# Pair 1 of a gated layer with seven down products, a normalisation moved to ScalarE, and four pages for stores

## The chip, the cores and the metric

The kernel runs on one core of one Trainium2 chip. The metric is the device time of one execution, in microseconds (us). Before the change the median of three runs is 809.46 us (809.42 to 809.92).

## The reference, cut to what matters

```
x  = A_x                                    # 2048 x 512
xn = (x - mean(x)) / sqrt(var(x) + 1e-5)    # along the 512
a, b = xn @ Wd_re.T, xn @ Wd_im.T           # 512 x 512
s  = Ws_re @ a - Ws_im @ b                  # 2048 x 2048
h  = sigmoid(xn @ w_gate) * (xn @ w_up)     # 512 x 1792, twice
g  = silu(h @ w_down)                       # 1792 x 512
out = x + s * g
```

All is fp32. The kernel is given x also turned (`x_t`), and writes its output turned.

## The kernel before, in words

Each fp32 operand is split into a high part (a copy to fp32r on ScalarE, line 71) and a low part (a subtraction on VectorE, line 72), and each product is three matmuls (`mm3`, lines 75 to 77). Most matrix products are done as 2 x 2 blocks with seven block products in place of eight, from sums and differences of blocks that VectorE makes (line 123, `combine`).

The 1792 columns of the gated layer are seven groups of 256, called pairs; the 2048 rows are two halves h of 1024. A *block* (h, g) is one pair for one half. `BLOCKS` (line 28) gives their order: `start` does (0, 0), and (0, 1) (0, 2) (0, 3) (0, 4) (1, 4) ... follow. A block (`block`, line 443) is seven *units*, one for each of the products 1, 5, 2, 6, 7, 4, 3 that make gate and up together; a unit is 12 matmuls of 512 columns, into PSUM banks ga, gb, gc (gate) and ua, ub, uc (up). Chain a is used by products 1, 6, 7, 4; between them ScalarE copies banks away: `snap` (line 454) after product 6, which is position 3 of the block, and after product 7, position 4. `gate` (line 469) is the sigmoid, `times` (line 472) its product with up, `plus` (line 464) adds bank c.

The product with `w_down` (the *down* of a block) runs during the next block, item by item, at the end of units, into the two banks pd. There are two ways. `Plain` (line 313) has 4 items at positions 1, 3, 4, 6, each 2 outputs x 2 halves x 3 matmuls. `Seven` (line 387) has 7 items, one at each unit, each 2 outputs x 3 matmuls; it needs more operands: four sums of gated blocks, seven splits of them, and `Down` (line 359): four differences of quarters of the weights and two splits of 1024. `late` makes `Down.spread` (line 382) come four units later. In the kernel before, the first half uses `Plain` for pairs 1 and 2 and `Seven` from pair 3 on (`SEVEN_FROM`, line 30); the second half uses `Seven` throughout. The down of a block is stored at once: `gather` (line 297) copies the two banks with ScalarE (line 301) into a page, and GpSimd's queue stores the page to the DRAM tile `g_part`, adding if something is there (line 303).

The first half of x is normalised in `start`. For the second half (tiles 8 to 15 of 128 rows, i >= KH), `norm_a` (line 156) makes the statistics on VectorE (lines 160, 161) and mean and scale on GpSimd (lines 165 to 167) into the tile `moments`; `norm_b` (line 170) normalises the tile on VectorE (line 172); `store_xn` (line 196) stores it to `xn_part` from GpSimd's queue. The same rows are needed turned: `turned_half` (line 174) stores the moments to DRAM (`m_part`, line 182), loads them spread over all partitions, loads the turned x, and applies subtraction and product on VectorE (line 187) in four steps for each of two blocks of 512 columns. `x_sum` (line 236) makes the sums of these for the second half.

What sets the order: the whole program is written in the order of the units, and each engine and queue runs its own instructions in that order. In the loop at line 1013, unit n first runs what `sooner(n, ..)` holds, then starts the loads that units up to n + 5 need (SP's queue), makes the split operands that units up to n + 2 need, issues its matmuls, and then runs what `after(n, ..)` holds. Here unit 0 is the first of block (0, 1); block (0, 2) is units 7 to 13, (0, 3) units 14 to 20, and `turned_at` (line 989) is unit 28. The places of the second half's work are numbers in lines 991 to 1005.

All working tiles in SBUF come from one pool of 54 *pages* of 4 KB a partition (line 43): loads, splits, sums, and what is stored. A page that is given again is waited for by its first writer until the last reader, a store among them, is through.

After the gated layer come the two DFTs (`seq_units`, `hidden_units`). `silu_ahead` (line 718) makes silu of `g_part` in two pages, and `snap` in `after_product` (line 797) copies banks of the sequence DFT.

Of the kernel before, what the change touches and what calls it, by code (L numbers as in the profile page):

```python
# [9 lines left out]
F32 = mybir.dt.float32  # L10
F32R = mybir.dt.float32r
AF = mybir.ActivationFunctionType
ALU = mybir.AluOpType
# [9 lines left out]
NT = S // 512  # L23
SB = 512
EPS = 1e-5
PAGES = 54
SCRATCH = 4096
BLOCKS = ((0, 1), (0, 2), (0, 3), (0, 4), (1, 4), (1, 5), (0, 5), (0, 6), (1, 6), (1, 0), (1, 1), (1, 2), (1, 3))
FIRST_TURNED = 1, 4
SEVEN_FROM = 3  # L30
SHARED = 4, 5, 6
SPLIT_AHEAD = 2
LOAD_AHEAD = 5

# [2 lines left out]
def fnet_glu_kernel(ctx: ExitStack, tc: tile.TileContext, x, x_t, c_re, c_im, w_h, w_gu, w_down, out):  # L37
# [3 lines left out]
    const = ctx.enter_context(tc.tile_pool(name="const", bufs=1))  # L41
    stat = ctx.enter_context(tc.tile_pool(name="stat", bufs=4))
    pages = ctx.enter_context(tc.tile_pool(name="pages", bufs=PAGES))
    dram = ctx.enter_context(tc.tile_pool(name="dram", bufs=1, space=bass.MemoryType.DRAM))
    banks = ctx.enter_context(tc.tile_pool(name="banks", bufs=1, space=PSUM))

    def page(shape, dtype=F32R):
        return pages.tile([P, *shape], dtype, name="page")

    def bank(tag):  # L50
        return banks.tile([P, 512], F32, name=tag, bufs=2 if tag == "pd" else 1)
# [6 lines left out]
    nc.gpsimd.memset(mhalf, -0.5)  # L58
    warm = const.tile([P, 1], F32, name="warm")
    nc.scalar.activation(warm, mhalf, AF.Sigmoid)  # L60
    moments = const.tile([P, 2, KH], F32, name="moments")
    m_part = dram.tile([2, 2, SB], F32, name="m_part")
    xn_part = dram.tile([2, 2, 2, P, 4, D // 2], F32, name="xn_part")
    g_part = [dram.tile([P, 2, SB], F32, name=f"g_part{i}") for i in range(2 * NT)]
# [91 lines left out]
    def norm_a(i):  # L156
        st = stat.tile([P, 6], F32, name="st")
        mv = stat.tile([P, 2], F32, name="mv")
        rs = stat.tile([P, 2], F32, name="rs")
        nc.vector.bn_stats(st, xs[i])  # L160
        nc.vector.bn_aggr(mv, st)
        mean, scale = mv[:, 0:1], rs[:, 1:2]
        if i >= KH:
            mean, scale = (moments[:, m, i - KH : i - KH + 1] for m in range(2))
            nc.gpsimd.tensor_scalar(mean, mv[:, 0:1], 0.0, None, op0=ALU.add)
        nc.gpsimd.tensor_scalar(rs[:, 0:1], mv[:, 1:2], EPS, None, op0=ALU.add)
        nc.gpsimd.tensor_tensor(scale, rs[:, 0:1], mhalf, op=ALU.pow)
        st_of[i] = mean, scale

    def norm_b(i):  # L170
        mean, scale = st_of.pop(i)
# [124 lines left out]

    def gather(i, outs, sign=1):

        pg = page([2, SB], F32)
        for o, po in enumerate(outs):  # L300
            nc.scalar.activation(pg[:, o, :], po, AF.Copy, scale=float(sign))  # L301
        if i in begun:
            nc.gpsimd.dma_start(g_part[i], pg, accum_op=ADD)  # L303
        else:
            begun.add(i)
            nc.gpsimd.dma_start(g_part[i], pg)
# [410 lines left out]

    def silu_ahead(n, i):
        g = Load(g_part[i], [2, SB])
        t = Value([g], lambda: page([2, SB], F32))  # L720

        def give():
            nc.gpsimd.dma_start(gs_part[i], combine(t.get(), t.get(), g.load(), ALU.mult))

        sooner(n, g.load)
        after(n + 2, lambda: nc.scalar.activation(t.get(), g.load(), AF.Sigmoid))
        after(n + 3, give)

    def seq_units(job, c_sums):
# [8 lines left out]
        for tc_ in range(NT):  # L738
# [29 lines left out]
            def after_product(k, n=n, tc_=tc_, ps=ps, s=s, made=made, first=first, tags=tags):  # L768
                def put(blk):
                    half, j = blk // 2 ^ 1, blk % 2  # L770
                    to = f_part[tc_ // 2, half]
                    if tc_ % 2 == 0 or j:
                        nc.gpsimd.dma_start(to[SLOT["ab"[j] if tc_ % 2 == 0 else 3]], made[blk])
                    if tc_ % 2 == 0 or j == 0:
                        return
                    a1, b1 = made[blk - 1], made[blk]
                    t2 = []

                    def total(k):
                        a0, b0 = (first[half, j].load() for j in range(2))  # L780
                        if k == 6:
                            t2.append(page([2, SB], F32))
                        v = {
                            5: lambda: combine(a0, a0, a1, ADD),
                            7: lambda: combine(a1, a1, b1, ADD),
                            6: lambda: combine(t2[0], a0, b1, ADD),
                            4: lambda: combine(b0, t2[0], b0, ADD),
                        }[k]()
                        nc.gpsimd.dma_start(to[SLOT[k]], v)

                    at = n + 25 if half == 0 else n + 28 + (9 if tc_ < NT - 1 else 4)
                    for j in range(2):
                        sooner(at - 4 + j, first[half, j].load)
                    for i, k in enumerate((5, 7, 6, 4)):
                        after(at + i, lambda k=k: total(k))

                def snap(name, ch):
                    s[name] = page([2, SB], F32)
                    for d in range(2):
                        nc.scalar.activation(s[name][:, d, :], ps[ch, d], AF.Copy)  # L800
                    return s[name]

                def join(blk, name, ch, op, swap=False):
                    made[blk] = v = s[name]
                    for d in range(2):
                        x, y = v[:, d, :], ps[ch, d]
                        nc.vector.tensor_tensor(v[:, d, :], *((y, x) if swap else (x, y)), op=op)
                    put(blk)

                if k == 1:  # L810
                    for d in range(2):
                        ps["b", d] = bank("gu"[d] + tags["b"])
                        nc.scalar.activation(ps["b", d], ps["a", d], AF.Copy)
                elif k == 5:
                    snap("u5", "c")
                elif k == 6:
                    snap("u2", "a")
                elif k == 3:
                    join(2, "u2", "c", SUB)
                elif k == 7:  # L820
                    join(3, "u5", "a", SUB, swap=True)
                elif k == 2:
                    made[0] = snap("u1", "b")
                    put(0)
                else:
                    made[1] = snap("u4", "a")
                    put(1)
# [151 lines left out]
    with tc.manual_schedule():  # L979
# [4 lines left out]
        for h, g in BLOCKS:  # L984
# [2 lines left out]
                w, wd, last = w_operands(g), Down(g), g  # L987
            if (h, g) == FIRST_TURNED:
                turned_at = len(units)
            job = block(h, w, made, job, Seven(h, wd, made) if h or g >= SEVEN_FROM else Plain(h, g), g in SHARED)  # L990
        for i in range(0, KH, 2):
            a, b = ((2, 9), (4, 10), (7, 12), (8, 14))[i // 2]
            if i >= 4:
                sooner(a - 4, lambda i=i: fetch(KH + i))
            for j in (i, i + 1):
                after(a, lambda j=j: norm_a(KH + j))
                after(b, lambda j=j: norm_b(KH + j))
                after(b + 1, lambda j=j: store_xn(KH + j))
        n = turned_at
        turned_half(4, 0, (n - 18, n - 17, n - 14, n - 4))  # L1000
        turned_half(8, 1, (n - 13, n - 12, n - 10, n - 3))
        for i, k in {-7: 1, -2: 2, 0: 3, 2: 4}.items():
            after(n + i, lambda k=k: x_sum(1, k))
        for i, k in {-8: 1, -5: 5, -2: 2, 0: 6, 1: 7, 3: 4}.items():
            sooner(n + i, xop[1, k].get)
# [72 lines left out]
```

## Time and profile before

| | |
|---|---|
| median of three runs | 809.46 us (809.42 to 809.92) |
| profiled execution: its own time | 809.49 us |
| profiled execution: span from first to last instruction | 807.7 us |
| granted clock of TensorE | 0.998 |
| instructions on TensorE | 3630 matmuls, 3630 weight loads |

The profile is of one execution. Its engines are PE (TensorE matmul), PEld (TensorE weight load), DVE (VectorE), ACT (ScalarE), POOL (GpSimd), and SP, whose queue issues the loads; SPq and POOLq are issues and waits on the queues. L71 is line 71 of the kernel. A row of a timeline has the start and length in us, the engine, line, operation and tiles, how many instructions were merged, and in brackets the idle time of the engine before it and what ended it. A row of groups has the count, the busy time in us and the mean of one in ns, and the idle time before. A row of stretches has for each engine the busy time and the number of instructions, then the granted clock, the share of the DMA engines and GB/s.

### The profile page before, as it was taken

Reading aid. Unit: us, or ns where it says so; the run is one execution under the profiler, and the core shown is the slowest. Engines: PE = TensorE matmul, PEld = TensorE weight load, DVE = VectorE, ACT = ScalarE, POOL = GpSimd, SP = SyncE. Lnnn points to the kernel's source line nnn. Section 1 sums busy time; section 2 is a strip of 40 time slices with the busy share of each in tenths; the row PEclk is TensorE's granted clock in tenths of the full one; section 3 lists DMA queues with packets and bytes.
Section 4 is the critical chain, followed back from the end, with each engine's and each line's share of the span. In section 5 each row is a group of like instructions: output and inputs, shape, how many; then the busy total and the mean of one; then the engine's idle time right before and its main releaser. Section 6 shows DMA issues by size and latency. Waiting matters only on the chain.

```text
span 807.7 us, 10264 instructions
## 1 busy us (share of the span) xinstructions
PE 800.6 (99%) x3630; PEld 665.2 (82%) x3630; DVE 639.7 (79%) x803; ACT 497.8 (62%) x761; POOL 148.6 (18%) x218
## 2 busy tenths in 40 slices
PE   9999999999999999999999999999999999999997
PEld 7988888888888888888888888888888888888886
DVE  6897879876776778887787897888888876986945
ACT  4674657777676778778777774445445545546360
POOL 3146321221222223122111100011101210001201
PEclk9999999999999999999999999999999999999999
DMA  8366983987899998998999878278919993699976
GB/s 276 143 222 118 240 239 67 185 160 153 258 251 225 297 275 160 225 219 181 233 281 333 223 223 285 81 284 298 328 79 334 348 374 142 253 338 381 309 255 104
DMA packets 54499, 189.42 MB, mean 235 GB/s; under 512 B 6192, under 2 KB 6448, under 8 KB 54448
## 3 DMA queue, kind: packets, MB, share of 16 engines
q0 software_dynamic: 24048, 83.38, 44.5%
q1 hardware_dynamic: 30320, 105.33, 36.8%
q8 instruction: 28, 0.46, 0.2%
q14 instruction: 23, 0.19, 0.1%
q10 hardware_dynamic: 80, 0.07, 0.0%
HBM read 108.53 MB, written 83.89 MB: 238 GB/s over the span
## 4 chain that ended last, share of the span: by engine, by line
PE 98%; DMA 1%; DVE 0%; ACT 0%; SPq 0%; issue 0%
PE pd L76 7%; PE pd L77 7%; PE pd L75 7%; PE ga L75 6%; PE ga L76 6%; PE ua L76 6%; PE ua L75 6%; PE ga L77 6%; PE ua L77 6%; PE gc L76 4%; PE uc L76 3%; PE uc L75 3%; PE gc L75 3%; PE gc L77 3%; PE uc L77 3%; PE ub L76 3%
## 5 line engine op out<-in xcount | busy, mean ns | idle before, releaser
L72 DVE TENSOR_TENSOR page<-page 128x1024 fp32r<-128x1024 f32 (+1 forms) x351 | 332.5, 976 | 110.7 <-ACT page L71 110.0
L71 ACT ACTIVATE page<-page 128x1024 fp32r<-128x1024 f32 (+1 forms) x351 | 284.3, 859 | 96.0 <-DVE page L123 78.7
L123 DVE TENSOR_TENSOR page<-page 128x1024 f32<-128x1024 f32 (+2 forms) x216 | 188.8, 894 | 0.6
L301 ACT ACTIVATE page<-pd 128x512 f32<-128x512 f32 x178 | 104.8, 598 | 63.1 <-PE pd L77 48.6
L303 POOL DMA_DIRECT2D g_part<-page x81 | 71.0, 906 | 290.1 <-ACT page L301 213.0
L75 PE MATMUL pd<-page 128*128 128x512 f32 x234 | 91.0, 389 | 0.0
L76 PE MATMUL pd<-page 128*128 128x512 f32 x234 | 91.0, 389 | 0.0
L77 PE MATMUL pd<-page 128*128 128x512 f32 x234 | 91.0, 389 | 0.0
L75 PE MATMUL ga<-page 128*128 128x512 f32 x200 | 78.1, 390 | 0.0
L76 PE MATMUL ga<-page 128*128 128x512 f32 x200 | 77.8, 389 | 0.0
L75 PE MATMUL ua<-page 128*128 128x512 f32 x200 | 77.8, 389 | 0.0
L77 PE MATMUL ga<-page 128*128 128x512 f32 x200 | 77.8, 389 | 0.0
L76 PE MATMUL ua<-page 128*128 128x512 f32 x200 | 77.8, 389 | 0.0
L77 PE MATMUL ua<-page 128*128 128x512 f32 x200 | 77.8, 389 | 0.0
L75 PEld LDWEIGHTS pd<-page 128*128 128x128 f32 x234 | 43.9, 188 | 9.2
L76 PEld LDWEIGHTS pd<-page 128*128 128x128 f32 x234 | 43.9, 188 | 9.1
L77 PEld LDWEIGHTS pd<-page 128*128 128x128 f32 x234 | 43.9, 188 | 9.1
L76 PE MATMUL gc<-page 128*128 128x512 f32 x124 | 48.4, 390 | 0.0
L77 PE MATMUL gc<-page 128*128 128x512 f32 x124 | 48.3, 389 | 0.0
L75 PE MATMUL uc<-page 128*128 128x512 f32 x124 | 48.2, 389 | 0.0
L75 PE MATMUL gc<-page 128*128 128x512 f32 x124 | 48.2, 389 | 0.0
L77 PE MATMUL uc<-page 128*128 128x512 f32 x124 | 48.2, 389 | 0.0
(132 smaller groups left out, 1298.2 us busy)
## 6 DMA issues: line engine op xcount, KB each, us to landing
g_part<-page POOLq DMA_DIRECT2D x89, 512.0 KB, 7.4
page<-f_part SPq DMA_DIRECT2D x36, 512.0 KB, 5.9
page<-in_c_re_dram SPq DMA_DIRECT2D x34, 512.0 KB, 5.9
page<-in_c_im_dram SPq DMA_DIRECT2D x33, 512.0 KB, 6.4
f_part<-page POOLq DMA_DIRECT2D x28, 512.0 KB, 5.9
page<-in_w_gu_dram SPq DMA_DIRECT2D x22, 512.0 KB, 6.7
page<-xn_part SPq DMA_DIRECT2D x14, 512.0 KB, 5.5
page<-in_w_down_dram SPq DMA_DIRECT2D x11, 512.0 KB, 7.5
```

Of the source, the lines that this page charges most:

```text
L71: nc.scalar.activation(hi, src, AF.Copy)
L72: nc.vector.tensor_tensor(lo, src, hi.bitcast(F32), op=SUB)
L75: nc.tensor.matmul(ps, ws[0], ms[0], start=first, stop=False, skip_group_check=go_on)
L76: nc.tensor.matmul(ps, ws[0], ms[1], start=False, stop=False, skip_group_check=go_on)
L77: nc.tensor.matmul(ps, ws[1], ms[0], start=False, stop=last, skip_group_check=go_on)
L123: (engine or nc.vector).tensor_tensor(dst, a, b, op=op)
L301: nc.scalar.activation(pg[:, o, :], po, AF.Copy, scale=float(sign))
L303: nc.gpsimd.dma_start(g_part[i], pg, accum_op=ADD)
```

## The change

- Pair 1 of the first half uses `Seven` in place of `Plain`, with the late places for its weights; only pair 2 stays `Plain`.
- The tiles of the second half are normalised by ScalarE: `second_norm` is one activation with scale and bias from `moments`, which gets a third row for the bias, -mean x scale; GpSimd makes it in two more small instructions a tile. `norm_b` is left for the first half alone.
- The places of statistics, normalisation and stores move, and with them the loads of the tiles. The steps and the moments' store and load of `turned_half`, and two sums of x, move too.
- Pages for stores of down products, for silu's product and for the copies of two of the four sequence blocks come from a pool of their own with four pages; the common pool has 50 in place of 54.

```diff
-PAGES = 54
+PAGES = 50
+SENT = 4
...
-SEVEN_FROM = 3
-SHARED = 4, 5, 6
+SEVENS = 1, 3, 4, 5, 6
+LATE = 1, 4, 5, 6
...
+    sent = ctx.enter_context(tc.tile_pool(name="sent", bufs=SENT))
...
+    def sent_page():
+        return sent.tile([P, 2, SB], F32, name="sent")
...
-    moments = const.tile([P, 2, KH], F32, name="moments")
+    moments = const.tile([P, 3, KH], F32, name="moments")
...
         nc.gpsimd.tensor_tensor(scale, rs[:, 0:1], mhalf, op=ALU.pow)
+        if i >= KH:
+            bias = moments[:, 2, i - KH : i - KH + 1]
+            nc.gpsimd.tensor_tensor(bias, mean, scale, op=ALU.mult)
+            nc.gpsimd.tensor_scalar(bias, bias, -1.0, None, op0=ALU.mult)
         st_of[i] = mean, scale
+
+    def second_norm(i):
+        scale, bias = (moments[:, m, i - KH : i - KH + 1] for m in (1, 2))
+        nc.scalar.activation(xs[i], xs[i], AF.Identity, scale=scale, bias=bias)
...
     def gather(i, outs, sign=1):
 
-        pg = page([2, SB], F32)
+        pg = sent_page()
...
-        t = Value([g], lambda: page([2, SB], F32))
+        t = Value([g], sent_page)
...
-                    s[name] = page([2, SB], F32)
+                    s[name] = page([2, SB], F32) if tc_ % 2 else sent_page()
...
-            job = block(h, w, made, job, Seven(h, wd, made) if h or g >= SEVEN_FROM else Plain(h, g), g in SHARED)
+            job = block(h, w, made, job, Seven(h, wd, made) if h or g in SEVENS else Plain(h, g), g in LATE)
         for i in range(0, KH, 2):
-            a, b = ((2, 9), (4, 10), (7, 12), (8, 14))[i // 2]
+            a, b = ((1, 5), (3, 9), (6, 13), (9, 15))[i // 2]
             if i >= 4:
                 sooner(a - 4, lambda i=i: fetch(KH + i))
             for j in (i, i + 1):
                 after(a, lambda j=j: norm_a(KH + j))
-                after(b, lambda j=j: norm_b(KH + j))
+                after(b, lambda j=j: second_norm(KH + j))
                 after(b + 1, lambda j=j: store_xn(KH + j))
         n = turned_at
-        turned_half(4, 0, (n - 18, n - 17, n - 14, n - 4))
-        turned_half(8, 1, (n - 13, n - 12, n - 10, n - 3))
-        for i, k in {-7: 1, -2: 2, 0: 3, 2: 4}.items():
+        turned_half(4, 0, (n - 16, n - 15, n - 13, n - 6))
+        turned_half(9, 1, (n - 12, n - 11, n - 10, n - 4))
+        for i, k in {-8: 1, -1: 2, 0: 3, 2: 4}.items():
             after(n + i, lambda k=k: x_sum(1, k))
```

## Prediction

> **What bounds the kernel now.** I read the page first, then the rate of TensorE (PE in the rows) by stage, then each place where it waited.
>
> ```profile
> span 807.7 us, 10264 instructions
> ...
> PE 800.6 (99%) x3630; PEld 665.2 (82%) x3630; DVE 639.7 (79%) x803; ACT 497.8 (62%) x761; POOL 148.6 (18%) x218
> ...
> PE 98%; DMA 1%; DVE 0%; ACT 0%; SPq 0%; issue 0%
> ```
>
> TensorE is busy nearly all the time and is 98% of the chain that ended last, so only the number of its instructions, and the few stalls, set the end. Busy time of pipelined matmuls doesn't show whether they run at full rate; their count in a stretch does. The second and third rows are two stretches that I need below: the block (0,2) as it runs now, and the block (0,4), in which seven-product downs already run at the shorter pace.
>
> ```profile
> 600.00:700.00 100.00, 100.00 (x442) 82.79 (x442) 82.03 (x75) 50.88 (x58) 11.99 (x20) 1.00 0.77 280
> 65.80:95.72 29.92, 29.92 (x133) 24.77 (x132) 22.60 (x39) 17.21 (x30) 14.18 (x22) 1.00 0.93 178
> 125.64:152.77 27.13, 27.13 (x121) 22.49 (x120) 23.59 (x36) 21.35 (x37) 5.16 (x6) 1.00 0.61 106
> ```
>
> The columns after the length are PE, weight loads, DVE (VectorE), ACT (ScalarE), POOL (GpSimd), the granted clock, DMA. 100 us hold 442 matmuls of 512 columns: **0.2262 us each**, at full clock. After the first 40 us I found three places where PE left this pace, in the timeline:
>
> ```profile
> 38.69 0.19 PEld L76 LDWEIGHTS gc<-page 128*128 128x128 f32 x1 [0.44 <-DVE page L72]
> ...
> 169.28 0.19 PEld L75 LDWEIGHTS ga<-page 128*128 128x128 f32 x1 [0.38 <-ACT page L454]
> ...
> 402.20 0.19 PEld L75 LDWEIGHTS ga<-page 128*128 128x128 f32 x1 [0.45 <-ACT page L454]
> ```
>
> The bracket is idle time of the weight-load unit, which is idle about 0.04 us in any case and can hide some; matmul starts around them slip by about 0.28, 0.23 and 0.30 us. So 0.8 us is all that can be won besides instructions. Two of the three wait for ScalarE's copy of bank ga (line 454, "snap"), which must be done before the next unit accumulates there: that is the place to watch.
>
> **What the change removes from TensorE.** A Plain down is 4 items of 2 outputs x 2 halves x 3 matmuls = 48; a Seven is 7 x 2 x 3 = 42. Pair 1 (block (0,1)) saves 6 matmuls, 6 x 0.2262 = **-1.36 us**, all on the path. Its items run in units 8 to 13 (block (0,2), units 7 to 13) and 14. Block (0,2) goes from 84 + 48 = 132 matmuls to 84 + 36 = 120, 29.9 to 27.1 us; unit 14 gains 6. So the other engines get 2.7 us less for that block, and more to do.
>
> **What it adds elsewhere**, priced by these groups (busy us, mean ns of one):
>
> ```profile
> L72 DVE TENSOR_TENSOR page<-page 128x1024 fp32r<-128x1024 f32 x190 | 227.6, 1221 | 87.7 <-ACT page L71 87.4
> ...
> L72 DVE TENSOR_TENSOR page<-page 128x512 fp32r<-128x512 f32 x161 | 106.2, 687 | 23.0 <-ACT page L71 22.6
> ...
> L123 DVE TENSOR_TENSOR page<-page 128x512 f32<-128x512 f32 x84 | 55.9, 686 | 0.4
> ...
> L160 DVE BATCH_NORM_STATS2 st<-page 128x6 f32<-128x512 f32 x16 | 10.9, 681 | 2.5 <-DMA page<-in_x_dram 2.5
> ...
> L161 DVE BATCH_NORM_AGGREGATE mv<-st 128x2 f32<-128x6 f32 x16 | 2.9, 182 | 0.8
> ...
> L172 DVE TENSOR_SCALAR page<-page,moments 128x512 f32<-128x512 f32 x8 | 4.0, 543 | 0.0
> ...
> L71 ACT ACTIVATE page<-page 128x1024 fp32r<-128x1024 f32 x190 | 192.1, 1055 | 70.7 <-DVE page L123 61.6 <-issue 5.0 <-DVE page L246 2.3
> L301 ACT ACTIVATE page<-pd 128x512 f32<-128x512 f32 x178 | 104.8, 598 | 63.1 <-PE pd L77 48.6 <-issue 8.9
> L71 ACT ACTIVATE page<-page 128x512 fp32r<-128x512 f32 x161 | 95.9, 627 | 25.3 <-DVE page L123 17.1 <-DVE page L472 6.1 <-DVE page L547 1.5
> ```
>
> VectorE in block (0,2): 22.60 now; minus six normalisations (3.26), minus the statistics of four tiles plus those of two (net -1.73: tiles 14 and 15 stay, in unit 9), minus two splits of the old down operands (1.37); the two steps at units 10, 11 go to 12, 13 (0). Plus four sums (2.74), six splits of 512 (4.12), the split of the weights' differences (1.22): **24.3 of 27.1 us, 90%**. Block (0,4) has 23.59 of 27.13 and no stall, so VectorE should hold; I put it at 0. Its price, if not: it has to finish operands two units ahead, so a unit's length (4.1 us) of lateness is spent before TensorE waits. Block (0,1) is nearly even on VectorE: two normalisation statistics move from unit 2 to 1 and from 4 to 3, two from 7 to 6, and the split of the raw weights from 3 to 6, four small differences come to 4 and 5.
>
> ScalarE in block (0,2): 17.21 now; minus two splits (1.25); plus six of 512 (3.76), one of 1024 (1.06), four more copies at line 301 (2.39), four normalisations. No row shows an ACTIVATE with scale and bias from memory; the nearest is the copy of the same shape, 0.63, and I take that; the ends are 0.54 (VectorE's row for the same work) and 1.06 (a copy twice as wide). 4 x 0.63 = 2.51: **25.7 of 27.1 us, 95%**, against 21.35 in block (0,4). Back-to-back instructions overlap, two copies take 1.14 and not 1.25, so it is nearer 85%; but ScalarE works in order and must wait for PE between. It becomes the tight engine. I walk the tightest place, units 9 and 10:
>
> ```profile
> 75.92 1.00 DVE L172 TENSOR_SCALAR page<-page,moments 128x512 f32<-128x512 f32 x2
> ...
> 78.30 0.60 ACT L454 ACTIVATE page<-ga 128x512 f32<-128x512 f32 x1 [1.60 <-PE ga L77]
> ...
> 89.55 1.14 ACT L71 ACTIVATE page<-page 128x512 fp32r<-128x512 f32 x2
> ```
>
> Now ScalarE stands idle 1.60 us before the snap. After: count from the end of unit 9's matmuls. The second copy of its down item starts 0.2 later and takes to 0.75; the gate (line 469) to 1.3; the two normalisations of tiles 10 and 11 to 2.4; two splits of 512 to 3.4; the snap of ga ends at 4.0. Unit 10 lasts 18 x 0.2262 = 4.07 us, and then unit 11 wants ga. Margin 0.1 us; at the ends of the normalisation's price, 0.3 of margin or 0.8 of stall. Unit 11 repeats this with the wide split of the raw weights of pair 2 (about 0.95) in place of the normalisations. I put **+0.3 us** for both together (0 to 1.2).
>
> On this the Trainium skill speaks against the change. Its page "ScalarE: Activation LUTs", section "What ACT_TABLE_LOAD costs", gives an ACTIVATE with immediates 186 ns + 0.833 ns an element, which is 0.61 us at 512 and agrees with the 0.627 of the row, and 93 ns more for each operand pointer; by that the normalisation would be 0.80 us, as an estimate, 0.35 more at unit 9, and the sum would be 808.9, inside the forecast's own range.
>
> GpSimd gets two small instructions for each of eight tiles. Line 167's like take 0.65, so at most 10 us in all on an engine that is 18% busy; ScalarE needs the bias four to seven units after the statistics: 0. Behind them on GpSimd's queue stand the stores of down products and of m_part. The second m_part store moves behind unit 9, whose product adds onto the tile that unit 8 wrote and so waits for that landing; its load, now asked for at unit 14, blocks SP's queue, and VectorE may wait for it in unit 16. The cover is this wait:
>
> ```profile
> 113.82 1.23 DVE L72 TENSOR_TENSOR page<-page 128x1024 fp32r<-128x1024 f32 x1 [4.25 <-ACT page L71]
> ```
>
> VectorE idles 4.25 us in unit 17 anyway, so up to 4 us are free: 0. The moved steps and sums of the turned tiles (x_sum 2 goes from unit 26 to 27) bring ScalarE's snap before 169.28 a little later: **+0.1** (-0.2 to +0.4).
>
> **Four pages for stores.** A page is filled by ScalarE and free when the store has landed; the fifth store then waits on ScalarE, in order, with the splits and snaps behind it. Units are 4.07 us, so four pages last 16.3 us.
>
> ```profile
> 275.05 1.28 ACT L301 ACTIVATE page<-pd 128x512 f32<-128x512 f32 x2
> ...
> 287.29 1.28 ACT L301 ACTIVATE page<-pd 128x512 f32<-128x512 f32 x2
> ...
> 303.67 1.22 ACT L301 ACTIVATE page<-pd 128x512 f32<-128x512 f32 x2
> ...
> 314.91 0.64 ACT L71 ACTIVATE page<-page 128x512 fp32r<-128x512 f32 x1 [0.39 <-DMA g_part<-page]
> ```
>
> ```profile
> 288.06 0.86 POOL L303 DMA_DIRECT2D g_part<-page  x1 [9.90 <-ACT page L301]
> ...
> 304.62 2.62 POOL L303 DMA_DIRECT2D g_part<-page  x3 [10.82 <-ACT page L301]
> 317.78 2.60 POOL L303 DMA_DIRECT2D g_part<-page  x3 [10.55 <-ACT page L301]
> ```
>
> These are the slowest stores. The named releaser had long been done: the issues at 288.06, 304.62 and 317.78 wait for an earlier store onto the same tile. Its copies started at 275.05, 287.29 and 303.67, so three pages took 13.0, 17.3 and 14.1 us. One exceeds 16.3, by 1.0; a copy may be 1.9 us late before PE wants the pd bank (12 matmuls, 2.7, less 0.2 and 0.6). So 0. The last ACT row shows the other side: today a split waits 0.39 us for a page that a store still holds, and that goes; but no stall follows from it, so 0 too.
>
> **Sum** on the profiled execution: 809.49 - 1.36 + 0.3 + 0.1 = 808.53; it stands 0.03 above the median, 809.46. I predict **808.5 us**.
>
> **Rivals.**
> 1. The old stalls go as well, since fewer normalisations weigh on VectorE and stores hold no pages: -1.36 - 0.28 - 0.23 - 0.30 = -2.17, 807.3. Against: the one at 38.69 is before the change begins, and before 402.20 nothing changes. Chance 0.10.
> 2. Slower, by the four pages: where stores take f us from copy to landing, the pace is f/4 a unit in place of 4.07. Over some 9 units around 280 to 316 us that costs 9 x (f/4 - 4.07) - 1.9. It outweighs the gain by over 1.6 us from f = 18.5 on; at 20 it is +6.5, 814.6. For: 17.3 in the rows. Against: the mean of the three is 14.8, and a late copy is partly hidden since the store waits for the earlier landing anyway. Chance 0.13.
> 3. ScalarE falls behind in units 8 to 15 for good: each of eight units loses half a us to a wait on VectorE, +4, 812.1. For: 95% by summed time. Against: overlap, and block (0,4). Chance 0.12.
> 4. The matmuls don't fall by 6: the code leaves no way, and the instruction count will tell; no chance of its own.
>
> **Numbers.** About 0.2% (1.6 us) is what a measurement of this kernel can tell from no change. The forecast, 0.65, has its own range 807.9 to 811.0: its bounds (0 to 1.2, -0.2 to +0.4, half a us of page waits, and 0.8 us of what I haven't seen). It lies within 0.2%, since -1.36 alone is 0.17%. Faster 0.10 (rival 1), within 0.2% 0.65, slower 0.25 (rivals 2 and 3). The range 807.8 to 812.2 takes in the forecast and rival 3 and leaves out rivals 1 and most of 2.
>
> **What would show it.** 3624 matmuls; the same 442 in 100 us; stalls only at snaps of ga near units 10 to 12 (about 80 to 86 us), at 38.69 and near 168 and 401. Idle time of ScalarE ended by a g_part store under 2 us at a time. Normalisations on ScalarE near 0.63 us. I am wrong if stalls of several us stand behind splits of VectorE in 65 to 110 us, or behind line 301 waiting for stores.

## The result and the profile after

The changed kernel takes 820.70 us (median of 4 executions, 819.99 to 822.60) against 809.46: a ratio of 1.0133, 95% interval 1.011 to 1.0156. It is 11.2 us **slower**. The forecast was 808.5, the range ended at 812.2, and "slower" had a chance of 0.25.

These are the lines of the changed kernel's page that answer to those of before: span, engines, the chain that ended last, and the stores of the down products.

```profile
span 818.7 us, 10247 instructions
...
PE 803.7 (98%) x3624; PEld 665.9 (81%) x3624; DVE 643.8 (79%) x807; ACT 506.5 (62%) x779; POOL 159.7 (20%) x237
...
PE 75%; DMA 13%; POOL 4%; issue 3%; DVE 3%; ACT 2%; SPq 0%; POOLq 0%; ACTq 0%; DVEq 0%
...
g_part<-sent POOLq DMA_DIRECT2D x92, 512.0 KB, 8.3
```

The six matmuls are gone (3624), but TensorE is no longer 98% of the chain. 13% of it are now transfers: something waited for stores to land (the chain runs back along earlier stores too, so the share is not the time lost). The windows say where. First come the stretches that were shown of before (100 us of steady work, block (0,2), block (0,4)), then the neighbourhood of the one place that differs.

```profile
612.00:712.00 100.00, 100.00 (x443) 82.84 (x442) 82.95 (x76) 53.55 (x60) 11.95 (x20) 1.00 0.73 275
65.75:93.31 27.56, 27.54 (x122) 22.44 (x121) 24.11 (x41) 22.86 (x41) 17.82 (x29) 1.00 0.77 161
134.29:161.49 27.20, 27.20 (x121) 22.52 (x120) 23.75 (x36) 21.77 (x37) 5.09 (x6) 1.00 0.66 104
...
92.00:100.00 8.00, 8.00 (x37) 6.52 (x35) 7.24 (x12) 5.74 (x10) 4.38 (x6) 1.00 1.12 32
100.00:107.00 7.00, 0.29 (x3) 0.02 (x1) 0.00 (x0) 0.67 (x2) 0.00 (x0) 0.68 0.74 164
...
107.00:110.00 3.00, 3.00 (x7) 2.42 (x8) 2.04 (x4) 1.45 (x3) 0.00 (x0) 0.50 1.03 264
110.00:113.00 3.00, 3.00 (x9) 2.28 (x9) 0.99 (x1) 1.09 (x3) 1.55 (x3) 0.55 1.05 280
113.00:120.00 7.00, 7.00 (x32) 5.76 (x31) 4.30 (x7) 4.70 (x9) 4.04 (x6) 1.00 1.06 290
```

The pace is as it was (443 in 100 us), and block (0,2) runs at the shorter pace as forecast. Then TensorE stands from 100 to 107 us with all engines nearly idle, and runs the next 6 us at about half the granted clock (0.50, 0.55; 7 matmuls in 3 us instead of 13). The row at 92 is the strangest: the DMA engines are shown as fully busy (1.12, the second last column) and move **32 GB/s** (the last), where the rows from 107 us on have 264 to 290, and the same stretch of before had 285:

```profile
92.00:100.00 8.00, 8.00 (x37) 6.63 (x36) 7.32 (x14) 5.77 (x11) 2.38 (x3) 1.00 1.02 285
```

Followed back through the timeline of the changed kernel, the stall looks so:

```profile
106.98 0.79 PE L80 MATMUL pd<-page 128*128 128x512 f32 x1 [6.71 <-ACT sent L314]
...
106.33 1.09 ACT L314 ACTIVATE sent<-pd 128x512 f32<-128x512 f32 x2 [8.01 <-DMA g_part<-sent]
...
81.20 1.10 ACT L314 ACTIVATE sent<-pd 128x512 f32<-128x512 f32 x2
...
84.60 0.86 POOL L316 DMA_DIRECT2D g_part<-sent  x1 [7.37 <-ACT page L76]
85.18 0.60 POOL L170 TENSOR_SCALAR moments<-mv 128x1 f32<-128x1 f32 x1
...
90.26 0.24 POOL L176 TENSOR_SCALAR moments<-moments 128x1 f32<-128x1 f32 x1
90.47 1.67 POOL L195 DMA_DIRECT2D m_part<-moments  x2
92.10 0.99 POOL L316 DMA_DIRECT2D g_part<-sent  x1
```

TensorE waits for a pd bank; ScalarE, which has to empty it into a page, waits 8.01 us for unit 10's store to land (106.25), which holds the page. That store's copy was made at 81.2 us. GpSimd issued it only at 92.10: it stood behind unit 9's store, which waited until unit 8's store onto the same tile had landed (84.07; the row names a split of ScalarE, but the issue follows the landing by 0.53, and by 0.53 again in `common54` and `vecnorm` below), then behind ten small steps for the last two tiles, then behind the two stores of their statistics. And once issued it took 14 us to land instead of the 8.3 of the page: from copy to landing 25.0 us, with 16.3 us of four units to spare.

The sum closes on the spans, 818.7 against 807.7: -1.36 for the matmuls; +6.88 for this stall; +2.80 for the matmuls behind it, of which 13 are each 0.2 us late or a little more; +0.30 at 80.89 us; +0.26 more than before at 178.19; +1.55 at 426.30 and 428.04; +0.37 in two small ones. That makes 10.80 of 11.0 us; the rest is spread in amounts too small to place.

### The profile page after: what moved, and what is told of

It is laid out like the page before. It is cut to its first block, busy times and chain, and to the rows that moved or that the text cites. A ratio compares the mean times of both kernels' runs of the same rounds, so it can differ in the third digit from the quotient of the medians.

```text
span 818.7 us, 10247 instructions
## 1 busy us (share of the span) xinstructions
PE 803.7 (98%) x3624; PEld 665.9 (81%) x3624; DVE 643.8 (79%) x807; ACT 506.5 (62%) x779; POOL 159.7 (20%) x237
## 4 chain that ended last, share of the span: by engine, by line
PE 75%; DMA 13%; POOL 4%; issue 3%; DVE 3%; ACT 2%; SPq 0%; POOLq 0%; ACTq 0%; DVEq 0%
DMA g_part<-sent 11%; PE pd L80 4%; PE ga L81 4%; PE ga L80 4%; PE pd L82 4%; PE pd L81 4%; PE ua L80 4%; PE ua L81 4%; PE ga L82 4%; PE ua L82 4%; PE ub L80 3%; PE ub L81 3%; PE ub L82 3%; PE gb L80 3%; PE gb L81 3%; PE gb L82 3%
## 5 line engine op out<-in xcount | busy, mean ns | idle before, releaser
L76 ACT ACTIVATE page<-page 128x1024 fp32r<-128x1024 f32 (+1 forms) x355 | 287.5, 858 | 104.3 <-DVE page L128 76.6
L128 DVE TENSOR_TENSOR page<-page 128x512 f32<-128x512 f32 (+2 forms) x216 | 183.4, 868 | 1.4 <-PE ua L81 0.4
L314 ACT ACTIVATE sent<-pd 128x512 f32<-128x512 f32 x184 | 106.4, 598 | 69.7 <-PE pd L82 31.8
L316 POOL DMA_DIRECT2D g_part<-sent x84 | 74.0, 997 | 297.5 <-ACT sent L314 121.5
L80 PEld LDWEIGHTS pd<-page 128*128 128x128 f32 x232 | 44.1, 190 | 16.3 <-ACT sent L314 7.1
L80 PE MATMUL gb<-page 128*128 128x512 f32 (+1 forms) x126 | 48.4, 384 | 0.0
L80 PE MATMUL uc<-page 128*128 128x512 f32 x124 | 48.3, 389 | 0.0
```

Source lines behind the costliest of these rows:

```text
L76: nc.scalar.activation(hi, src, AF.Copy)
L80: nc.tensor.matmul(ps, ws[0], ms[0], start=first, stop=False, skip_group_check=go_on)
L128: (engine or nc.vector).tensor_tensor(dst, a, b, op=op)
```

## The experiments

The first four runs had three theories. **A**: four pages are too few. **B**: stores go out late, because of what stands in front of them on GpSimd's queue. **C**: the normalisation on ScalarE and its steps on GpSimd.

**Stores take common pages** (`common54`).

```
-PAGES = 50                          +PAGES = 54
-    sent = ctx.enter_context(...)
-        return sent.tile([P, 2, SB], F32, name="sent")
+        return page([2, SB], F32)
```

> All of the change but its pages: stores, silu and the copies take their pages from the common pool of 54 again. Theory A (four pages are too few: ScalarE waits for a landing, TensorE behind it): the stall of 6.9 us before unit 15's down item, the 2.6 us of slow clock behind it and the 1.5 us near 426 go, 820.7 falls to 808.5 to 809.5, so the rest of the change is worth -1 us or so. Theory B (the stores land late because of what stands in front of them on GpSimd's queue): the same time, but the store of unit 10 still takes over 20 us from copy to landing. Theory C (the normalisation on ScalarE and its steps on GpSimd are the cause): a stall of over 4 us stays between 90 and 115 us, 814 or more.

Measured: 819.23 us, ratio 1.0097 (1.0064 to 1.0129). The stall is there, 6.96 us at 107.2, and the row of ScalarE is the same with another page's name:

```profile
106.56 1.08 ACT L313 ACTIVATE page<-pd 128x512 f32<-128x512 f32 x2 [8.10 <-DMA g_part<-page]
```

Pages of the common pool come round again after about four units here, too, so a store that takes 25 us holds ScalarE up from either pool. A falls as the cause of the long stall. The waits at 426 and 428 are gone: these belong to the four pages.

**Six pages for stores, 48 common** (`six48`: `SENT = 6`, `PAGES = 48`).

> Six pages for stores and 48 common ones in place of 4 and 50. Theory A: with two more pages the copy of unit 14 takes the page of unit 8, landed at 84, and that of unit 90 takes the page of unit 84, landed at 409: no wait on ScalarE that TensorE sees, 808.5 to 809.5. If instead the common pages are what is short now, 48 are worse than 50: loads come late between 200 and 240 and 540 and 560 us, and it is over 810. Theory C: stays at 814 or more.

Measured: 841.16 us, ratio 1.0369 (1.0328 to 1.041). The stall became 11.75 us, since now a split of ScalarE waits for a common page that a store of normalised tiles holds, in the same queue behind the same statistics:

```profile
109.83 0.63 ACT L76 ACTIVATE page<-page 128x512 fp32r<-128x512 f32 x1 [12.85 <-DMA xn_part<-page]
```

48 common pages are too few elsewhere as well (stalls of 0.8 to 2.7 us at 213 to 255, and four of 1.1 at 551 to 563). As a test of A it is spoilt by that, but whichever page is scarce, the wait ends with a landing of that queue.

**The last statistics one unit sooner** (`early4`: tiles 14 and 15 at unit 8 instead of 9, their store with them, so ahead of unit 9's waiting store).

```
-  a, b = ((1, 5), (3, 9), (6, 13), (9, 15))[i // 2]
+  a, b = ((1, 5), (3, 9), (6, 13), (8, 15))[i // 2]
...
-  turned_half(9, 1, (n - 12, n - 11, n - 10, n - 4))
+  turned_half(8, 1, (n - 12, n - 11, n - 10, n - 4))
```

> The whole change with four pages, but the statistics of the last two tiles and the second moments store go back from unit 9 to unit 8, in front of the store that waits for unit 8's landing. Theory B: the moments store is issued near 83 and not 90.5, the stores of units 10 to 12 land before 101 and not at 106 to 115, the stall at 107 falls from 6.9 us to under 1.5 and with it the slow clock; about 1.5 us near 426 stay: 809.5 to 811.5. Theory A alone (four pages are short whatever is in front): the stall stays over 4 us, 816 or more.

Measured: 816.27 us, 811.82 to 819.51, ratio 1.0068 (1.0043 to 1.0093). The profiled execution stands at the low end; in it the long stall is three short ones, 0.94 at 82, 0.39 at 98, 0.70 at 103 us, and the clock stays up. The median misses the 809.5 to 811.5 of B by 5 us, and no profile shows the longer executions. The order on the queue matters (for B), but does not account for all.

**The pages alone** (`pagesonly`: the kernel before with four pages of their own, 50 common).

> The kernel before with four pages for stores and 50 common ones, nothing else. Theory A: ScalarE waits for landings between 290 and 320 us and near 410 to 425, TensorE loses 0 to 3 us there, 809.5 to 812.5. Theory B: nothing at 100 to 115 us, because stores come every 5.4 us there with Plain downs and unit 9 has none; the big stall needs the change's order. If pages alone made the whole loss: 818 or more.

Measured: 812.94 us, ratio 1.0024 (1.0002 to 1.0046). Nothing at 100 to 115 us; stalls of 0.62 at 317 and of 1.04 and 0.25 at 418 to 420. So the pages cost about 2 us by themselves (0.2 to 3.7 by the interval); in the change it was the 1.55 at 426 to 428.

The second four had a theory more. **D**: the statistics go out as single 4-byte words, which hold the DMA engines while 32 GB/s are moved. The expectations call these words packets; the profile does not show them one by one, but as 16 records of 128 bytes a store.

**Four words together** (`packets`).

```
-  m_part[b, m].rearrange("(o p) -> p o", p=P)
+  m_part[b, m].rearrange("(p o) -> p o", p=P)
```

> The changed kernel with the statistics stored as four neighbouring words a partition (16 bytes a packet, 256 packets) in place of single words (4 bytes, 1024 packets); the order of the words in memory is then another, so the means and scales reach the wrong columns of the turned tiles. Theory D, new: the store of the statistics holds all 16 DMA engines with 4-byte packets (share 1.22 and 1.02 at 34 and 30 GB/s in 92 to 100 us), so the stores issued with it land some 9 us late. D expects its landing to fall from 10 to about 3 us, unit 10's store to land before 101 instead of 106.25, the stall before unit 15's down item to fall from 6.9 us to under 1.5, no slow clock behind it, and 811 to 813 us. Theory B, the order on GpSimd's queue alone: issue times stay, unit 10's store is still issued near 92.1 and lands in the usual 10 us, at 102; stall about 2.7, 814 to 815. Theory C, the normalisation on ScalarE: nothing of it changes, stall near 7, 820.

Measured: 810.00 us (808.96 to 812.43), ratio 1.0001 (0.9989 to 1.0013): the whole 11 us gone with one line. (This kernel leaves out putting the words back in order, so the turned tiles get the scales of other columns; the work is the same.) No stall at 107, no low clock. The statistics land after 1.8 to 6.3 us, and the stretch that moved 32 GB/s moves 238; window and landing row of this run:

```profile
92.00:100.00 8.00, 8.00 (x37) 6.61 (x36) 7.15 (x13) 7.32 (x14) 2.33 (x3) 1.00 1.01 238
...
DMA to landing us min/median/max: 1.8/4.2/6.3
```

The same row of the changed kernel was:

```profile
DMA to landing us min/median/max: 9.5/10.8/11.8
```

The packet records of the changed kernel show what the engines did meanwhile: the 32 records of the second pair of statistics stores took 0.13 to 0.20 us each, but 4 KB packets of the stores behind them took **up to 7.7 us**, where 0.16 is the least; with four words together the longest took 1.7.

**The statistics' store behind three more stores** (`behind`: after unit 12, with the turned steps at units 18, 19, 20, 24).

> The changed kernel with the second store of the statistics after unit 12 in place of unit 9, so behind the stores of units 10 to 12, and the steps of the turned half at units 18, 19, 20 and 24. D expects the stall at 107 us to fall under 1.5 us, since nothing of 4 bytes is in flight from 85 to 95; the stores of units 13 to 15 are issued behind it and land late instead, with a stall of 0 to 3 us near 120; 811 to 815 us. B expects 1.7 us less of a stall (the two issues of 0.8 that stood before unit 10's store), 5.2 us, 818.5. C expects near 7 us, 820.

Measured: 826.07 us, ratio 1.0191 (1.0173 to 1.0209), over all three forecasts. As D said, the stall at 107 is gone (0.33 at 114), and the slow stretch has moved with the store:

```profile
104.00:112.00 8.00, 8.00 (x37) 6.62 (x36) 3.16 (x6) 4.39 (x8) 3.89 (x5) 1.00 1.21 56
```

But I had not followed the load. It is asked for at unit 14, waits on SP until the statistics have landed, and the weights of pair 2 stand behind it; TensorE then waits 13.6 us at 133.

```profile
113.83 0.33 SPq L91 DMA_DIRECT2D page<-m_part  x1
...
131.30 0.69 DVE L128 TENSOR_TENSOR page<-page 128x512 f32<-128x512 f32 x1 [14.57 <-DMA page<-in_w_gu_dram]
```

**Pair 1's down products as four items again** (`plain`: `SEVENS = 3, 4, 5, 6`, `LATE = 4, 5, 6`).

> The changed kernel with pair 1's down products as four items of two outputs again (48 matmuls, 3630 in all): four stores in units 8, 10, 11 and 13 instead of one in every unit, none onto a tile that the store before it wrote; everything else of the change stays. B and D expect no stall of over 1 us at 95 to 115 (the statistics still take 10 us to land, but no fifth store is due then), and 811 to 813 us, which is the time with pages alone. C expects that ScalarE, which keeps the four normalisations of this block, still makes unit 15 late by some us: over 815.

Measured: 811.84 us, ratio 1.0009 (0.9992 to 1.0026). No stall at 95 to 115, though the statistics still take 11.3 to 12.8 us to land: their store goes out at 81.13, no store waits for the one before it, and one is due every 5 to 8 us. ScalarE still does all normalisations, though in a block that is longer again. In `packets` it does them in the shorter block, and no stall stands at 107. So the normalisation itself is not the cause; the steps on GpSimd that C had beside it are for the next run.

**Normalisation on VectorE, no bias steps** (`vecnorm`: `norm_b` in place of `second_norm`, lines 173 to 176 left out).

> The changed kernel with the second-half tiles normalised on VectorE again, at the same places in the order, and without the two GpSimd steps for each bias: six instead of ten small steps stand between unit 9's store and the statistics' store. C expects the stall at 107 us to go: 811 to 812 us. B expects it shorter by the 2.1 us of four steps, 4.8 us: 818. D expects the same 5 to 7 us, since the 4-byte packets stay and move 2 us ahead at most: 817 to 820. All expect the small stall at 80.89 us (0.30), which stands at ScalarE's snap after two normalisations of 0.80, to go.

Measured: 813.98 us (810.82 to 816.50), ratio 1.0045 (1.0028 to 1.0062). None of the three had it: in the profiled execution, one of the shortest of ten, the stall shrinks from 6.88 to 2.35.

```profile
86.25 1.64 POOL L191 DMA_DIRECT2D m_part<-moments  x2
87.88 0.97 POOL L312 DMA_DIRECT2D g_part<-sent  x1
...
102.58 0.50 PE L80 MATMUL pd<-page 128*128 128x512 f32 x1 [2.19 <-ACT sent L310]
```

Unit 10's store goes out at 87.88 instead of 92.10, 4.2 us sooner, and the stall is 4.5 shorter. The edit takes two things away at once, but the queue points to the bias steps, which cost "0" in my sum: four of them stood directly ahead of the store, four more ahead of unit 8's store, for which unit 9's waits. Unit 8's store goes out at 74.65 in place of 76.25, although its copy is made 0.5 us later, and unit 9's at 81.95 in place of 84.60. The small stall at 81, which all three theories expected to go, stays (0.30 and 0.11): ahead of the same snap ScalarE now waits for a sum that VectorE makes behind its normalisations.

```profile
79.87 0.63 ACT L76 ACTIVATE page<-page 128x512 fp32r<-128x512 f32 x1 [1.41 <-DVE page L128]
```

The next four tried for a better kernel with the words stored four together: `wide54` reads the words back in order with two strided VectorE instructions a step and has 54 common pages, `wide54v` normalises on VectorE as well; `before16` is the kernel before with this diff alone, `early54` has single words, the early statistics of `early4` and common pages.

```
-  m_part[b, m].rearrange("(o p) -> p o", p=P)
+  m_part[b, m].rearrange("(p o) -> p o", p=P)
...
-  by = both.load()[:, m, :].unsqueeze(1).to_broadcast([P, 2, SB])
-  nc.vector.tensor_tensor(v, v, by, op=(SUB, ALU.mult)[m])
+  by = both.load()[:, m, :].rearrange("q (p o) -> q o p", p=P)
+  for d in range(2):
+      w = v[:, d, :].rearrange("q (o p) -> q o p", p=P)
+      nc.vector.tensor_tensor(w, w, by, op=(SUB, ALU.mult)[m])
```

> The changed kernel with the statistics stored as 16-byte packets, four words of a partition together, and the turned steps reading them back in that order (two VectorE instructions of 512 in place of one of 1024); stores take common pages, 54 in all. D expects no stall over 1 us at 95 to 115, none near 312 to 330 and 426 (those belong to the four pages), and the six matmuls show: 809.46 - 1.36 + 0.3 (snap at 81) + 0 to 1.0 (small waits near 235) = 808.3 to 809.5. If the late landing has another cause than the packets (B), a stall of 2 us or more stays at 107: 810.5 or more. C: near 817.

> The same, with the second-half tiles normalised on VectorE at the same places and without the two GpSimd steps for each bias. Against the run before it this gives the price of the normalisation on ScalarE where no stall of the stores hides it: C expects 2 us or more less; D expects 0 to 0.5 us less (the 0.3 at the snap near 81): 808.0 to 809.2.

> The kernel before with the 16-byte packets alone. In it no store is late enough to hold anything, so D expects no difference: 809.5 within 0.3. If the packets themselves slowed TensorE in some other way, 0.5 us or more would go.

> The changed kernel with the last two tiles' statistics and their store one unit sooner, in front of unit 9's waiting store, in 4-byte packets as in the change, and with 54 common pages. With four pages of their own the same order left stalls of 0.94 at 82, 0.39 at 98 and 0.70 at 103. B (the order on the queue decides) expects those at 98 and 103 to go: 809.0 to 810.0. D expects them to stay, since the packets still hold the DMA engines from 84 to 92 and pages come round again after about four units in either pool: 810.0 to 811.5.

| | median us | ratio, 95% interval |
|---|---|---|
| wide54 | 810.86 | 1.0010 (1.0000 to 1.0020) |
| wide54v | 809.94 | 1.0000 (0.9992 to 1.0009) |
| before16 | 810.45 | 0.9999 (0.9985 to 1.0013) |
| early54 | 812.26 | 1.0027 (1.0013 to 1.0040) |

`before16` shows that the wider words win nothing by themselves: in the kernel before no store is late enough. `early54` keeps one of the two stalls, 1.21 us at 102, as D said and B didn't (the one at 98 is down to 0.08), with a time a little above both. Neither wide version has a stall at 107, but they miss the ends of their forecasts by 1.4 and 0.7 us (the kernel before, run with them, took 810.05). Most of that is of my own making: reading with a stride makes a turned step 2 x 1.08 us (the group below, of `wide54v`) instead of 1.22, and TensorE waits 0.73 and 0.11 at 140, after the step of unit 24.

```profile
L197 DVE TENSOR_TENSOR page<-page 128x512 f32<-128x512 f32 x16 | 16.6, 1078 | 0.0
```

In `wide54v` that 0.84, 0.37 at 81 and 0.32 more than before at 169 make 1.53: the matmuls' 1.36 went there. `wide54` takes 0.92 us more than `wide54v`, between the 0.5 that D allowed for the normalisation on ScalarE and the 2 of C. But the stalls that `wide54` has more stand at 431 and 439 us, far from any normalisation, so what costs it is open.

**Half the words at a time** (`split54`, `split54v`: two tiles' statistics stored at units 1, 3, 6, 9) and **only the seven products** (`sevenonly`: the kernel before with pair 1 as Seven, spread late, and nothing else).

```
-  def store():
-      at = slice(b * SB // P, (b + 1) * SB // P)
+  def store(k):
+      at = slice(b * SB // P + 2 * k, b * SB // P + 2 * k + 2)
...
-  after(n, store)
+  for k in range(2):
+      after(n[k], lambda k=k: store(k))
...
-  turned_half(9, 1, (n - 12, n - 11, n - 10, n - 4))
+  turned_half((6, 9), 1, (n - 12, n - 11, n - 10, n - 4))
```

```
-  Seven(h, wd, made) if h or g >= SEVEN_FROM else Plain(h, g), g in SHARED
+  Seven(h, wd, made) if h or g >= SEVEN_FROM or g == 1 else Plain(h, g), g in SHARED or g == 1
```

> The changed kernel with the statistics stored tile pair by tile pair, half as soon as two tiles have theirs (units 1 and 3, units 6 and 9), still in 4-byte packets, and 54 common pages: behind unit 9's store 512 packets are issued in place of 1024. D expects their landing to take about 5 us instead of 10 and the stall at 107 us (7.0 in the run with common pages) to be 4 to 5 us shorter: 2 to 3 us left, hardly a slow clock behind it, 811 to 812.5. B (order alone): one issue of two stores stays where it was, stall 6 to 7, 817 to 819.

> The same with the second-half tiles normalised on VectorE and without the two GpSimd steps for each bias, which made the stores go out 4.2 us sooner in the run with that edit alone. D and B together add up: 7.0 - 4.5 - 4.2, so no stall at 107; left are the snaps at 81 and 169 (0.3 and 0.4) and small waits near 235: 808.5 to 809.5. If this is not at least as fast as the kernel before, the six matmuls are lost to something that I have not named.

> The kernel before with only pair 1's down products made as seven, and their operands spread late: statistics, their store (after unit 8), normalisation on VectorE and 54 common pages as before. Unit 9's store waits for unit 8's landing with nothing in front of it but the statistics' store, which now goes out ahead of it as in the run with the earlier statistics: D expects a stall of 0.5 to 2 us near 102 and VectorE, with four sums and eight more splits in block (0,2) on top of six normalisations, up to 1 us late: 809.5 to 811.5. A gain (808.5) would say that the rest of the change was not needed; over 813 that VectorE, not ScalarE, is the engine that the six matmuls overload.

Measured: `split54` 828.50 (ratio 1.0218, 1.0196 to 1.024), `split54v` 824.79 (1.0183, 1.016 to 1.0206), `sevenonly` 815.09 (1.0062, 1.0041 to 1.0083). D as it stood fell with the first: half as many words land no sooner (landing row of `split54`), and GpSimd now gets stuck twice, stalls of 2.8 at 83 and 10.8 at 113. `split54v`, forecast at 808.5 to 809.5, has 2.6 at 83 and 9.3 at 108.

```profile
DMA to landing us min/median/max: 9.6/10.7/18.4
```

`sevenonly` shows that the rest of the change isn't needed for the trouble: the seven products alone cost 5 us of the 11 by the median. The profiled execution, the slowest of six, has a stall of 4.47 us at 90.79 and 13 slow matmuls behind it. I had thought of VectorE; the row says ScalarE, held by a store's page as before.

```profile
90.14 0.60 ACT L454 ACTIVATE page<-ga 128x512 f32<-128x512 f32 x1 [4.65 <-DMA g_part<-page]
```

If not the number, then perhaps the place of the words: **E**, words next to each other, written at once from several partitions into one stretch of 64 bytes, wait for one another. `spaced` adds to `packets` a second pair of stores of the same 1024 single words, each 64 bytes from the next, into a place that nobody reads.

```
+  pad = dram.tile([2, 2, SB, 16], F32, name="pad")
...
+  nc.gpsimd.dma_start(pad[b, m, :, 0:1].rearrange("(o p) w -> p o w", p=P),
+                      moments[:, m, at].unsqueeze(2))
```

> The run with 16-byte packets (statistics in another order, so the scales reach the wrong columns) with a second pair of stores right behind them: the same 1024 words as 4-byte packets, each into a stretch of 64 bytes of its own in a place that nobody reads. If every small packet has its price (D as it stood, 1024 of them about 10 us), they land in about 10 us, 4 KB packets issued behind them take 3 to 8 us as in the changed kernel, and the stall at 107 us comes back with 4 to 7 us: 815 to 820. If the price is in neighbouring words written at once into the same stretch (E, to which it fits that half as many words took as long), they land in 2 to 5 us and no stall over 1.5 us stands at 95 to 115: 810 to 813.

Measured: 811.74 us, ratio 1.0013 (0.9993 to 1.0033), with 1.85 us of a stall at 102, where E had put at most 1.5; unit 10's store goes out 1.5 us later than without these stores. They are as many and as small as those of the change, and land in half the time:

```profile
L198 POOL DMA_DIRECT2D pad<-moments x4: 760/771/795, 63.1 to 90.8; - x4
...
DMA to landing us min/median/max: 3.2/5.1/7.2
```

Of the 4 KB packets issued behind them until 107 us none took over 1.0 us, against 7.7 in the change. So the place decides, not the number. Whether 64 bytes is the stretch that counts was not tested, and why neighbouring words are slow is not shown.

**The words put back in order once** (`wide54r`: `wide54v`, with one VectorE copy a half, so that the steps are as in the change).

```
+  if not told:
+      told.append(page([2, SB], F32))
+      for k in range(2):
+          to = told[0][:, k, :].rearrange("q (o p) -> q o p", p=P)
+          nc.vector.tensor_copy(to, both.load()[:, k, :].rearrange("q (p o) -> q o p", p=P))
+  by = told[0][:, m, :].unsqueeze(1).to_broadcast([P, 2, SB])
```

> The version with 16-byte packets, 54 common pages and VectorE's normalisation, in which one VectorE copy of 2 x 512 puts the statistics back in order once a half, so that the turned steps are one instruction of 1024 again (1.22 us in place of 2.08): 2.1 + 4 x 1.2 = 7.0 instead of 8.3 a half, and the step in unit 24 is short again. If the turned steps are where the six matmuls went, the stall at 140 (0.73 and 0.11) goes and 808.7 to 809.4 is left, 0.5 to 1.2 below the same run without the copy; if not, it stays at 809.9.

Measured: 809.81 us (808.98 to 810.31), ratio 0.9985 (0.9970 to 1.0000). The stall at 140 is gone, but the time is 0.4 above the end of the forecast. It is the best version by this ratio, 0.15% ahead of the kernel before (0.07% by the medians), and the interval ends at no difference, so a gain is not shown. The profiled execution has waits of 0.35 at 431 and 0.53 at 438 us, as `wide54` has (0.08 and 0.59), so the matmuls' full 1.36 isn't had.

## Why the prediction was wrong, step by step

- **The matmuls, -1.36 us**: right. 3624, at the same pace.
- **VectorE, 0**: right. It was to be busy 24.3 us in block (0,2) and was 24.11; no stall there waits for it.
- **ScalarE and the snap of ga, +0.3**: the size and the place were right (0.30 us at 80.89, in unit 11), and so was the block's share (22.86 of 27.56 us, 83%, where I had said nearer 85%). The price of a normalisation was not: the row below gives 0.81 us, two in 1.52, where the walk had 1.1. The 0.80 that followed from the Trainium skill's page "ScalarE: Activation LUTs", section "What ACT_TABLE_LOAD costs", agrees, and my 0.63, from the copy without operands in memory, was too low. The 0.4 more, less the walk's margin of 0.1, is the 0.30 measured; my 0.3 was a middle put for two units, and that the two agree is in part luck.

```profile
L181 ACT ACTIVATE page<-page,moments 128x512 f32<-128x512 f32 x8 | 6.1, 808 | 0.0
```

- **GpSimd's bias steps, "0"**: the first failed step. Their time was inside its bound (5.4 us for all sixteen, of at most 10). But an engine that is mostly idle can still be late with one thing: they stand in order ahead of stores that hold pages. `vecnorm` prices that at 4.5 us of the stall, in one execution of each.
- **The second m_part store behind unit 9, "0"**: the second failed step, and the decisive one. I followed it to its load, to SP and to VectorE, and not to the stores issued with it. The trace of before had the warning, in its DMA issues from 60 to 125 us: 2 KB that take as long as 512 KB.

```profile
g_part<-page POOLq DMA_DIRECT2D x8, 512.0 KB, 9.9
...
m_part<-moments POOLq DMA_DIRECT2D x4, 2.0 KB, 10.8
```

In before these stores go out at 79.58, and the profile names no wait for a landing between 60 and 125 us, so that the slowness cost nothing. `packets` shows that with faster words the rest of the lateness is covered. The place behind unit 9 is not all of it: `sevenonly` has the statistics after unit 8, as before, and no bias steps, and still loses 5 us.

- **+0.1 at 169**: +0.26, inside its ends.
- **Four pages, "0"**: I bounded the time from copy to landing by rows of 275 to 318 us (17.3 at most), another stage; at 81 to 115 us it is 25.0 to 25.8. Rival 2 had the mechanism, a copy of ScalarE that waits in order for a landing, but as a price on each of nine units near 280 to 316 us and from too few pages. It was one wait of 8.0 us at 106, and it comes with 54 common pages too. That is the last of the signs that the prediction named for being wrong: the copy of line 301 (line 314 now) waiting for a store. The pages' own price is the 1.55 at 426 to 428.
- **The clock** was in no term: 2.80 us.

Single edits take away more than their share here, since the delays add up before a cushion: without the bias steps the stall is 2.35, with four words together nothing is left, without the extra stores (`plain`) nothing either. The long stall has three things at once: a store in every unit, a queue on GpSimd that runs late (by a store that waits for the one before it, and by small steps), and slow landings. Without the small steps a shorter one is left (`vecnorm`, `sevenonly`); without a store in every unit (`plain`) or with quick landings (`packets`) there is none at that place.

## What to carry to other kernels

A store's page is busy from the copy that fills it to the landing, so follow every edit on the issuing engine's queue to the transfers behind it, in the stage where it stands, even if that engine is idle 80% of the time. Look at transfers whose landing takes long for their size: they are the ones that make others late, and regrouping their words can be worth more than moving them. When a tuned kernel is given shorter work in one stage, its cushions shrink with the work.

## What the runs showed of the hardware

- Stores of single neighbouring 4-byte words (2 KB a store) took about 11 us to land (9.5 to 11.8 in the changed kernel), and 4 KB packets behind them up to 7.7 us; half as many words took as long (9.6 to 18.4); the same words 64 bytes apart took 3.2 to 7.2, four words together 1.8 to 6.3. The Trainium skill's page "DMA: Bandwidth & Descriptors", section "Specifications", says that transfers under 512 bytes are read, modified and written back. That fits neighbours that wait for each other, but the quicker stores here are of small pieces too; no run here shows the cause.
- A stall of TensorE can cost more than itself. After single waits of 2.35 (`vecnorm`), 2.61 (`split54v`) and 2.68 us (`six48`) the clock stayed full; after 2.82 (`split54`) five matmuls, after 4.47 (`sevenonly`) and 6.88 (the change) thirteen each came at about 0.43 us. A length alone does not tell: in `six48` the clock also fell (0.50 from 234.5 to 236 us, seven matmuls), behind waits of 1.79 and 1.92 us with six matmuls at full clock between them. The Trainium skill's page "TensorE: Matmul & The Clock Gate", section "What's actually happening", puts this at an idle window of about 3.4 us, which isn't aligned with the stall; the waits of 4.47 and 6.88 agree, the 2.82 and the pair in `six48` lie below.
- A VectorE instruction that reads every fourth word took 1.08 us for 512 elements (`wide54v`), against 0.69 for sums of 512 read in a row (line 123 before).
